# Two buffers by turns for the 16-bit tops of layer 1's weights

## The chip, the cores and the metric

The kernel runs on one core of a Trainium2 chip. Its time is the device time of one execution in microseconds (us); three runs of the kernel before gave 930.24, 930.90 and 930.96, median 930.9. Each engine of the core works through a queue of its own, in order: TensorE (PE in the rows; PEld is its weight loads), VectorE (DVE), ScalarE (ACT), GpSimd (POOL) and SyncE (SP), which only issues DMAs here. An instruction that waits holds up all that stands behind it on its engine.

## The reference

An attention block with exponential features, and behind it two feed-forward layers, each 512 to 2048 to 512 wide, over 2304 tokens:

```
q_p, k_p = phi(q_s), phi(k_s)          # phi(x) = exp(h - max(h)) / sqrt(m), h = x omega^T - |x|^2/2
num = q_p (k_p^T v);  den = q_p sum(k_p);  x = num / den       # 4 batches x 8 heads, 576 tokens
h = x @ w_in;  x = (h * clip(h + 3, 0, 6) / 6) @ w_out         # layer 1
h = x @ w_in;  out = (h / (1 + exp(-1.702 h))) @ w_out         # layer 2
```

## The kernel before

**Weights.** The weights reach the kernel as 64-bit floats, laid out in 16 chunks for each layer; a chunk holds 128 columns of w_in ("i") and 128 rows of w_out ("o"). For each chunk the kernel makes 32-bit floats, and splits these into a rounded part and a rest, since TensorE multiplies every product as three rounded ones. In the code l = 0 is layer 1 and l = 1 is layer 2. The conversion of a chunk is a chain over four engines:

- `convert_1`: ScalarE takes the top 16 bits of each word into `wtop` (L183) and the middle 32 bits into `w` (L185). VectorE works on `wtop` (L187 into `wmag`, L191 in place, L195 into `wpow`). GpSimd multiplies `w` by `wpow`, in two halves (L200).
- `convert_2`: VectorE adds `wtop` to `w` (L207), ScalarE rounds the half (L210), VectorE takes the rest (L211). The first half is the chunk's w_in, the second its w_out. L207 is the last reader of `wtop`.

`wtop` is a tile of 128x1024 16-bit values with a tag; tiles of one tag share its buffers. For l = 0 the tag is `wtop0` for every chunk, with one buffer, so L183 of a chunk can't start until both L207 of the chunk before are done. For l = 1 the tags `wtop0` and `wtop1` alternate. `wmag` and `wpow` have one buffer, `w`, the raw chunk `wraw` two, and the split weights go to a ring of six buffers (`wss`) or to eight that are kept (`wsh`).

**The work around it.** Layer 1 is done by 16 units for each batch: `emit_h` of a chunk is twelve products of 128x512 (L506), whose result ScalarE and VectorE gate and split into `gs` (L517, L518, L522, L523), and `emit_o` two units later adds the chunk's part of the output, twelve products (L556). Batch 0's units run while the weights are converted for the first time, two chunks ahead in the program's text; between them TensorE has the attention of batch 1 (projections L256, transposes L380, L432 and L439, L358 and L394 for the sums and quotients, with norms on VectorE, L416 to L421, and features, L267 and L269). The last quarter of a batch's attention reaches layer 1 through L432, L250 (ScalarE) and L251 (VectorE), which write the rows of `x` that every unit's last three products read.

**What sets the order.** The order on each engine is not the order of the text: when the program is built, a scheduler goes through a timeline of its own and lets each engine take what is ready there. So a change of buffers can move instructions on every engine, up to where the two timelines meet again.

Of the kernel before, what the change touches and what calls it, by code (L numbers as in the profile page):

```python
# [13 lines left out]
BF16 = mybir.dt.bfloat16  # L14
# [8 lines left out]
def performer_moe_kernel(  # L23
# [18 lines left out]
    B, NPAIR, P = qk.shape[:3]  # L42
# [25 lines left out]
    wp = wctx.enter_context(tc.tile_pool(name="wp", bufs=1))  # L68
# [23 lines left out]
    def behind(*ins):  # L92
        stack = ExitStack()
        for i in ins:
            if i is not None:
                stack.enter_context(tc.issue_after(i.ins))
        return stack
# [72 lines left out]
    def convert_1(l, c, act=None, dve=None):  # L170
        t = wraw.pop((l, c)).rearrange("p (w s) -> p w s", s=4)
        n = 2 * DM
        top = t[:, 1:n + 1, 0]
        mid = t.rearrange("p w s -> p (w s)").bitcast(U32).rearrange("p (w s) -> p w s", s=2)[:, 0:n, 1]
        a = wp.tile([P, n], BF16, tag=f"wtop{l and c % 2}", bufs=1, name="wtop")
        m = wp.tile([P, n], BF16, tag="wmag", bufs=1, name="wmag")
        q = wp.tile([P, n], BF16, tag="wpow", bufs=1, name="wpow")
        w = wp.tile([P, n], F32, tag="w", bufs=2, name="w")

        ab, mb, qb = a.bitcast(I32), m.bitcast(I32), q.bitcast(I32)  # L180
        act = act if isinstance(act, tuple) else (act, act)
        with behind(act[0]):
            nc.scalar.activation(out=a, in_=top.bitcast(BF16), func=AF.Copy, scale=2.0 ** -112)  # L183
        with behind(act[1]):
            nc.scalar.activation(out=w, in_=mid, func=AF.Copy, scale=2.0 ** -36)  # L185
        with behind(dve):
            nc.vector.tensor_scalar(  # L187
                out=mb, in0=ab, scalar1=3, scalar2=0x7FF87FF8,
                op0=ALU.logical_shift_left, op1=ALU.bitwise_and,
            )  # L190
            nc.vector.scalar_tensor_tensor(  # L191
                out=ab, in0=ab, scalar=-0x7FFF8000, in1=mb,
                op0=ALU.bitwise_and, op1=ALU.bitwise_or,
            )
            nc.vector.tensor_scalar(  # L195
                out=qb, in0=ab, scalar1=-0x7F0080, scalar2=None, op0=ALU.bitwise_and
            )
        for j in range(2):
            cols = slice(j * DM, (j + 1) * DM)
            nc.gpsimd.tensor_tensor(out=w[:, cols], in0=w[:, cols], in1=q[:, cols], op=ALU.mult)  # L200
        half[l, c] = a, w
# [512 lines left out]
    def convert_next(stage, upto, act=None, dve=None):  # L714

        while n_conv[stage - 1] < min(upto, len(conv)):
            if stage == 1:
                prefetch_w()
                convert_1(*conv[n_conv[0]], act, dve)
            else:  # L720
                convert_next(1, n_conv[1] + 1, act, dve)
                convert_2(*conv[n_conv[1]])
            n_conv[stage - 1] += 1
        prefetch_w()
# [96 lines left out]
    for u in range(len(units) + LAG):  # L821
        while fetches and fetches[0][0] <= u + AHEAD:
            fetch_w(0, *fetches.pop(0)[1:])
        if u < len(units):
            n, c = units[u]
# [373 lines left out]
```

## Time and profile before

| | us |
|---|---|
| median of the runs | 930.9 |
| the profiled execution | 930.89 |
| its span, first to last instruction | 929.1 |
| TensorE busy | 914.1 (98%) |
| VectorE, ScalarE, GpSimd busy | 585.9, 481.5, 334.4 |
| granted TensorE clock | 1.00, in every slice of the span |

Batch 0's units of layer 1 with the conversion of layer 1's weights take the stretch from about 36 to 176 us; before it stands the attention of batch 0, behind it the units of batches 1 to 3, then layer 2. An engine's busy time counts what its instructions hold, also where two matmuls overlap or an instruction is held up while it runs. A number in square brackets behind a row is idle time of the engine, with what ended it.

### The profile page before, as it was taken

Reading aid. Unit: us, or ns where it says so; the run is one execution under the profiler, and the core shown is the slowest. Engines: PE = TensorE matmul, PEld = TensorE weight load, DVE = VectorE, ACT = ScalarE, POOL = GpSimd, SP = SyncE. Lnnn points to the kernel's source line nnn. Section 1 sums busy time; section 2 is a strip of 40 time slices with the busy share of each in tenths; the row PEclk is TensorE's granted clock in tenths of the full one; section 3 lists DMA queues with packets and bytes.
Section 4 is the critical chain, followed back from the end, with each engine's and each line's share of the span. In section 5 each row is a group of like instructions: output and inputs, shape, how many; then the busy total and the mean of one; then the engine's idle time right before and its main releaser. Section 6 shows DMA issues by size and latency. Waiting matters only on the chain.

```text
span 929.1 us, 16457 instructions
## 1 busy us (share of the span) xinstructions
PE 914.1 (98%) x6274; PEld 782.1 (84%) x6274; DVE 585.9 (63%) x980; ACT 481.5 (52%) x977; POOL 334.4 (36%) x283
## 2 busy tenths in 40 slices
PE   8999999999999999999999999999999999999998
PEld 6877777778887888878888888878999888899997
DVE  5888889587585766727643433766875443377653
ACT  6977676476665665636533333444544223244443
POOL 0122222077573547544772112784000244420000
PEclk9999999999999999999999999999999999999999
DMA  6677777889878887766765426999889654566672
GB/s 210 241 250 250 238 248 268 293 297 339 307 271 277 287 319 288 261 238 234 265 239 191 137 93 224 369 405 316 275 285 333 199 175 159 176 187 183 169 261 92
DMA packets 75167, 228.77 MB, mean 246 GB/s; under 512 B 7504, under 2 KB 13264, under 8 KB 75088
## 3 DMA queue, kind: packets, MB, share of 16 engines
q1 hardware_dynamic: 74928, 227.45, 71.2%
q8 instruction: 50, 0.82, 0.3%
q10 hardware_dynamic: 160, 0.26, 0.1%
q14 instruction: 29, 0.24, 0.1%
HBM read 164.77 MB, written 62.91 MB: 245 GB/s over the span
## 4 chain that ended last, share of the span: by engine, by line
PE 84%; DVE 9%; ACT 3%; POOL 2%; issue 1%; DMA 1%; POOLq 0%; DVEq 0%; ACTq 0%
PE o L1003 19%; PE ps L506 18%; PE o L556 18%; PE h L872 16%; PE ps L261 3%; PE hl L889 2%; DVE w L207 2%; PE ps L394 1%; PE ps L256 1%; PE ps L358 1%; DVE gs L523 1%; PE ps L380 1%; POOL w L200 1%; DVE wtop L191 1%; ACT e L269 1%
## 5 line engine op out<-in xcount | busy, mean ns | idle before, releaser
L506 PE MATMUL ps<-x,wss 128*128 128x512 f32 x768 | 193.9, 397 | 3.3 <-ACT wss L210 1.8
L1003 PE MATMUL o<-wss,gs 128*128 128x256 f32 x1536 | 185.4, 283 | 0.3
L1003 PEld LDWEIGHTS o<-wss,gs 128*128 128x128 f32 x1536 | 184.6, 191 | 1.2 <-DVE gs L974 0.5
L506 PEld LDWEIGHTS ps<-x,wss 128*128 128x128 f32 x768 | 139.4, 188 | 35.4 <-ACT wss L210 3.7
L872 PE MATMUL h<-xo,wss 128*128 128x512 f32 x672 | 160.0, 394 | 0.4 <-DVE t L905 0.4
L200 POOL TENSOR_TENSOR w<-w,wpow 128x512 f32<-128x512 f32 x64 | 78.1, 1240 | 202.1 <-DVE wpow L195 123.6
L872 PEld LDWEIGHTS h<-xo,wss 128*128 128x128 f32 x672 | 124.1, 188 | 28.1 <-DVE t L905 0.8
L913 POOL TENSOR_TENSOR g<-g,c 128x512 f32<-128x512 f32 x48 | 64.5, 1346 | 170.3 <-ACT g L912 170.0
L973 ACT CAST gs<-g 128x512 fp32r<-128x512 f32 x112 | 69.4, 621 | 85.1 <-PE o L1003 79.3
L556 PE MATMUL o<-gs,wsh 128*128 128x512 f32 (+1 forms) x480 | 111.7, 377 | 0.3 <-ACT gs L522 0.3
L556 PE MATMUL o<-gs,wss 128*128 128x512 f32 (+1 forms) x480 | 109.4, 374 | 2.4 <-ACT gs L522 2.4
L974 DVE TENSOR_TENSOR gs<-g,gs 128x512 fp32r<-128x512 f32 x112 | 79.7, 716 | 47.8 <-ACT gs L973 45.0
L224 POOL TENSOR_TENSOR wsn<-w,wsn 128x512 fp32r<-128x512 f32 x64 | 90.5, 1429 | 48.8 <-ACT wsn L223 48.8
L518 DVE SCALAR_TENSOR_TENSOR ga<-ga,ps 128x512 f32<-128x512 f32 (+1 forms) x80 | 50.0, 629 | 91.3 <-ACT ga L517 91.1
L517 ACT ACTIVATE ga<-ps,three 128x512 f32<-128x512 f32 (+1 forms) x80 | 51.6, 650 | 94.1 <-PE ps L506 93.9
L556 PEld LDWEIGHTS o<-gs,wss 128*128 128x128 f32 x480 | 81.5, 188 | 17.3 <-ACT gs L522 3.3
L556 PEld LDWEIGHTS o<-gs,wsh 128*128 128x128 f32 x480 | 81.7, 188 | 16.2 <-ACT gs L522 1.0
L269 ACT ACTIVATE e<-ps,mx 128x128 f32<-128x128 f32 x220 | 62.2, 392 | 30.9 <-DVE mx L267 30.9
L523 DVE TENSOR_TENSOR gs<-ga,gs 128x512 fp32r<-128x512 f32 (+1 forms) x80 | 65.1, 824 | 19.4 <-ACT gs L522 18.1
L207 DVE TENSOR_TENSOR w<-w,wtop 128x512 f32<-128x512 f32 x64 | 65.5, 1033 | 10.6 <-POOL w L200 10.2
L912 ACT ACTIVATE g<-c 128x512 f32<-128x512 f32 x48 | 30.3, 632 | 60.3 <-DVE c L905 60.3
L223 ACT CAST wsn<-w 128x512 fp32r<-128x512 f32 x64 | 38.6, 626 | 27.3 <-issue 9.5
(146 smaller groups left out, 1184.1 us busy)
## 6 DMA issues: line engine op xcount, KB each, us to landing
wss<-left SPq DMA_DIRECT2D x64, 512.0 KB, 4.0
wss<-ws0i SPq DMA_DIRECT2D x48, 512.0 KB, 4.6
wraw<-in_w_in_dram SPq DMA_DIRECT2D x32, 512.0 KB, 4.8
wraw<-in_w_out_dram SPq DMA_DIRECT2D x32, 512.0 KB, 5.9
left<-wsn SPq DMA_DIRECT2D x32, 512.0 KB, 3.6
wss<-ws0o SPq DMA_DIRECT2D x24, 512.0 KB, 4.4
ws0i<-wss SPq DMA_DIRECT2D x16, 512.0 KB, 3.1
wss<-sumsa SPq DMA_DIRECT2D x16, 512.0 KB, 3.9
```

What stands on the lines that cost most here:

```text
L200: nc.gpsimd.tensor_tensor(out=w[:, cols], in0=w[:, cols], in1=q[:, cols], op=ALU.mult)
L207: nc.vector.tensor_tensor(out=wj, in0=wj, in1=a[:, j * DM:(j + 1) * DM], op=ALU.add)
L224: nc.gpsimd.tensor_tensor(out=s[:, :, 1], in0=t, in1=s[:, :, 0].bitcast(F32), op=ALU.subtract)
L269: act = nc.scalar.activation(out=e[:, r, :], in_=ps[:, r, :], func=AF.Exp, bias=mx[:, r:r + 1])
L506: nc.tensor.matmul(out=ps, lhsT=w[:, wi, kk, :], rhs=x[:, xi, kk, :], start=(m == 0), stop=(m == 3 * NK - 1),)
L523: gate[1] = nc.vector.tensor_tensor(out=s[:, 1, :], in0=g, in1=s[:, 0, :].bitcast(F32), op=ALU.subtract)
L556: nc.tensor.matmul(out=ps[:, e, :], lhsT=w[:, wi, cols], rhs=s[:, gi, :], start=(c == 0 and m == 0 and per == 1), stop=(c == NC - 1 and m ...
L872: nc.tensor.matmul(out=ps, lhsT=s[:, wi, q, :], rhs=xop[q, op][:, xi], start=(first and m == 0), stop=(m == 5), skip_group_check=not first,)
L913: mul = eng.tensor_tensor(out=g, in0=g, in1=src, op=ALU.mult)
L973: split_ins[0] = nc.scalar.copy(s[:, 0], g)
L974: split_ins[1] = nc.vector.tensor_tensor(out=s[:, 1], in0=g, in1=s[:, 0].bitcast(F32), op=ALU.subtract)
L1003: last_row[0] = nc.tensor.matmul(out=out, lhsT=s[:, gi, d * P:(d + 1) * P], rhs=w[:, wi, :], start=(start and m == 0), stop=(stop and m == 2),
```

## The change

The tag of `wtop` alternates for both layers, instead of for layer 2 alone. The second buffer exists already.

```
-        a = wp.tile([P, n], BF16, tag=f"wtop{l and c % 2}", bufs=1, name="wtop")
+        a = wp.tile([P, n], BF16, tag=f"wtop{c % 2}", bufs=1, name="wtop")
```

No instruction is added or removed; the scheduler's order changes on TensorE, VectorE, ScalarE and SyncE between about 37 and 178 us of the span before, and is the same from there to the end. GpSimd's is the same throughout.

The first place is TensorE's queue in the opening, where batch 0's attention ends. `ps_800`, `ps_889` and `ps_954` are the results of units 0, 1 and 2, `xt_726` the last quarter of batch 0's attention, `x0_196` layer 1's input. Before:

```order
L506 MATMUL ps_889<-x0_196,wss_880 128x512 x7
L256 MATMUL ps_908<-omt_166,qk_647 128x128 x4
L432 MATMUL acc_786<-ident_81,xt_726 128x128 x4
L439 MATMUL acc_793<-ident_81,xln_316 128x64 x3
L256 MATMUL ps_909<-omt_166,qk_647 128x128 x4
L439 MATMUL acc_793<-ident_81,xln_316 128x64
L506 MATMUL ps_800<-x0_196,wss_626 128x512
L506 MATMUL ps_889<-x0_196,wss_880 128x512
L506 MATMUL ps_800<-x0_196,wss_626 128x512 x2
L506 MATMUL ps_889<-x0_196,wss_880 128x512 x2
L506 MATMUL ps_954<-x0_196,wss_946 128x512 x12
```

After:

```order
L506 MATMUL ps_889<-x0_196,wss_880 128x512 x7
L256 MATMUL ps_909<-omt_166,qk_647 128x128 x4
L432 MATMUL acc_786<-ident_81,xt_726 128x128 x4
L439 MATMUL acc_793<-ident_81,xln_316 128x64 x3
L506 MATMUL ps_954<-x0_196,wss_946 128x512 x9
L506 MATMUL ps_800<-x0_196,wss_626 128x512
L506 MATMUL ps_889<-x0_196,wss_880 128x512
L506 MATMUL ps_954<-x0_196,wss_946 128x512
L439 MATMUL acc_793<-ident_81,xln_316 128x64
L380 MATMUL ps_973<-ident_81,e_829 128x128 x4
L506 MATMUL ps_800<-x0_196,wss_626 128x512 x2
L506 MATMUL ps_889<-x0_196,wss_880 128x512 x2
```

The four projections into `ps_908` stand ahead of the seven products now, those into `ps_909` ahead of the transposes; nine products of unit 2 come ahead of the ones that need the last rows of `x`. Behind this TensorE now has all of unit 3 and eight more projections before the first L556; before, the first L556 came ahead of unit 3.

The second place is VectorE's queue around the norm of that last quarter (`xt_726` from `den_776`), in the same opening. `wtop_931` and `w_934` belong to chunk 2, `wtop_980` to chunk 3. Before:

```order
L416 TENSOR_SCALAR den_776<-acc_765 128x4
L420 RECIPROCAL rden_778<-den_776 128x4
L187 TENSOR_SCALAR wmag_932<-wtop_931 128x512
L421 TENSOR_TENSOR xt_726<-acc_765,rden_778 128x4x64
L416 TENSOR_SCALAR den_781<-acc_765 64x2
L191 SCALAR_TENSOR_TENSOR wtop_931<-wtop_931,wmag_932 128x512
L420 RECIPROCAL rden_783<-den_781 64x2
L195 TENSOR_SCALAR wpow_933<-wtop_931 128x512
L421 TENSOR_TENSOR xln_316<-acc_765,rden_783 64x128
```

After:

```order
L416 TENSOR_SCALAR den_776<-acc_765 128x4
L211 TENSOR_TENSOR wss_885<-w_868,wss_885 128x512
L207 TENSOR_TENSOR w_934<-w_934,wtop_931 128x512
L420 RECIPROCAL rden_778<-den_776 128x4
L187 TENSOR_SCALAR wmag_981<-wtop_980 128x512
L267 TENSOR_REDUCE mx_919<-ps_908 128x4
L207 TENSOR_TENSOR w_934<-w_934,wtop_931 128x512
L421 TENSOR_TENSOR xt_726<-acc_765,rden_778 128x4x64
L416 TENSOR_SCALAR den_781<-acc_765 64x2
L191 SCALAR_TENSOR_TENSOR wtop_980<-wtop_980,wmag_981 128x512
L211 TENSOR_TENSOR wss_946<-w_934,wss_946 128x512
L267 TENSOR_REDUCE mx_925<-ps_909 128x4
```

The conversion stands a whole step further on at the same point: chunk 2 has its L207 here where it had its L187, and chunk 3 its L187. L191 and L195 of chunk 2 are further up now.

The third place is TensorE's queue in the middle of the stretch, at a unit in the second half of the 16. Before:

```order
L380 MATMUL ps<-ident,e 128x128 x4
L556 MATMUL o<-gs,wss 128x512 x12
L506 MATMUL ps<-x_196,wss 128x512 x2
L358 MATMUL ps<-v,e 64x65 x8
L366 MATMUL ps<-lv,el 64x65
L506 MATMUL ps<-x_196,wss 128x512 x10
```

After:

```order
L380 MATMUL ps<-ident,e 128x128 x4
L556 MATMUL o<-gs,wsh 128x512 x10
L506 MATMUL ps<-x_196,wss 128x512 x12
L358 MATMUL ps<-v,e 64x65 x8
L366 MATMUL ps<-lv,el 64x65 x2
```

Before, the first two products of a unit, which need only L210's rounded half of the weights, stand apart from the ten that need L211's rest too, with attention between them. After, the twelve of a unit follow each other.

## Rows read from the trace of the kernel before

**Rows 1.** The page: busy us of each engine, share of the span, instructions.
```profile
PE 914.1 (98%) x6274; PEld 782.1 (84%) x6274; DVE 585.9 (63%) x980; ACT 481.5 (52%) x977; POOL 334.4 (36%) x283
```

**Rows 2.** Windows: stretch and its length, each engine's busy us (instructions), clock, DMA share.
```profile
44.00:59.00 15.00, 14.58 (x111) 10.74 (x107) 13.23 (x29) 13.68 (x34) 2.33 (x3) 1.00 0.87 288
...
74.00:174.00 100.00, 95.90 (x680) 73.48 (x681) 84.82 (x157) 67.58 (x133) 25.12 (x22) 1.00 0.76 261
...
205.00:480.00 275.00, 274.85 (x1857) 225.69 (x1857) 176.60 (x293) 161.09 (x340) 168.60 (x151) 1.00 0.79 280
```

**Rows 3.** Waits of PE, 44 to 180 us: us in total, times, longest.
```profile
PE o L556 <- ACT gs L522: 2.7, 5, 1.2
PE ps L506 <- ACT wss L210: 1.8, 3, 1.2
PE ps L506 <- DVE wss L211: 0.4, 1, 0.4
```

**Rows 4.** Waits of PEld, 44 to 180 us.
```profile
PEld o L556 <- ACT gs L522: 4.3, 6, 1.4
PEld ps L506 <- ACT wss L210: 3.7, 5, 1.6
...
PEld ps L506 <- DVE wss L211: 0.9, 1, 0.9
```

**Rows 5.** Lines, PE, 44 to 180 us: busy, mean ns of one | idle before.
```profile
L506 PE MATMUL ps<-x,wss 128*128 128x512 f32 x195 | 52.4, 404 | 2.3 <-ACT wss L210 1.8 <-DVE wss L211 0.4
```

**Rows 6.** The chain of waits, 44 to 180 us: start, us, what.
```profile
76.30 2.74 PE ps L506 x12
```

**Rows 7.** Timeline of DVE, one chunk: start, us, instruction [idle before <-releaser].
```profile
143.89 0.43 DVE L187 TENSOR_SCALAR wmag<-wtop 128x512 int32<-128x512 int32 x1 [0.34 <-ACT wtop L183]
...
145.08 0.43 DVE L195 TENSOR_SCALAR wpow<-wtop 128x512 int32<-128x512 int32 x1
146.85 1.63 DVE L207 TENSOR_TENSOR w<-w,wtop 128x512 f32<-128x512 f32 x1 [1.34 <-POOL w L200]
...
149.00 0.68 DVE L207 TENSOR_TENSOR w<-w,wtop 128x512 f32<-128x512 f32 x1
149.60 0.68 DVE L211 TENSOR_TENSOR wss<-w,wss 128x512 fp32r<-128x512 f32 x1
```

**Rows 8.** Timeline of POOL, the same chunk.
```profile
145.65 2.28 POOL L200 TENSOR_TENSOR w<-w,wpow 128x512 f32<-128x512 f32 x2 [5.23 <-DVE wpow L195]
```

**Rows 9.** Timeline of ACT: L183 of this chunk and of the next.
```profile
142.73 1.13 ACT L183 ACTIVATE wtop<-wraw 128x1024 bf16<-128x1024 bf16 x1
...
150.24 1.11 ACT L183 ACTIVATE wtop<-wraw 128x1024 bf16<-128x1024 bf16 x1
```

**Rows 10.** Timeline of PE in the opening: last transposes of batch 0, first L556.
```profile
50.60 0.66 PE L432 MATMUL acc<-ident,xt 128*128 128x128 f32 x4
...
58.90 0.50 PE L556 MATMUL o<-gs,wsh 128*128 128x512 f32 x1
```

**Rows 11.** Timeline of DVE in the opening.
```profile
48.21 0.40 DVE L187 TENSOR_SCALAR wmag<-wtop 128x512 int32<-128x512 int32 x1
48.52 0.42 DVE L421 TENSOR_TENSOR xt<-acc,rden 128x256 f32<-128x256 f32 x1
...
51.91 0.69 DVE L251 TENSOR_TENSOR x<-acc,x 128x512 fp32r<-128x512 f32 x1 [0.51 <-ACT x L250]
```

**Rows 12.** Timeline of POOL where layer 2's weights are converted.
```profile
257.10 2.48 POOL L200 TENSOR_TENSOR w<-w,wpow 128x512 f32<-128x512 f32 x2 [5.70 <-DVE wpow L195]
```

**Rows 13.** Timeline of DVE, the same place.
```profile
257.41 1.14 DVE L187 TENSOR_SCALAR wmag<-wtop 128x512 int32<-128x512 int32 x1 [0.45 <-ACT wtop L183]
258.58 1.54 DVE L191 SCALAR_TENSOR_TENSOR wtop<-wtop,wmag 128x512 int32<-128x512 int32 x1
```

**Rows 14.** Timeline of PE, the projections of two heads of batch 1.
```profile
81.88 1.71 PE L256 MATMUL ps<-omt,qk 64*128 64x128 f32 x16
...
111.93 1.16 PE L256 MATMUL ps<-omt,qk 64*128 64x128 f32 x16
```

## The prediction

> **What bounds the kernel now.** I read the page first: TensorE is busy 98% of the span, so only its waits can be won [rows 1]. Next the windows: from 205 to 480 us it is busy 274.85 of 275, in the 100 us from 74 to 174 only 95.90, and there VectorE is at 84.82, in the opening (44 to 59) at 13.23 of 15 [rows 2]. The order is the same behind about 178 us, so whatever is gained or lost arises before that, and as TensorE is full afterwards it should reach the end unchanged.
>
> Then the waits of that stretch, twice. TensorE's matmuls sat idle 2.7 us for `gs` (five times) and 1.8 + 0.4 for the weights `wss` (four times), 4.9 in all [rows 3]. Its weight loads sat idle 4.3 + 3.7 + 0.9 = 8.9 for the same releasers [rows 4]. The truth lies between: a matmul counts as busy for 404 ns [rows 5], while in a full run of twelve one starts each 2.74 / 12 = 0.228 us [rows 6]; so each wait hides about 0.17 us in the busy time of the matmul before it. Nine waits give 4.9 + 9 x 0.17 = 6.4; I take 6.5. That is all there is to win here, 0.7% of the time.
>
> Last the timeline of one chunk. L183 starts at 142.73, L207's second half starts at 149.00, and the next chunk's L183 at 150.24, right behind it [rows 7, 9]. So a chunk is a chain of 7.5 us with no overlap with the next. On it VectorE idles 1.34 us for GpSimd and then its first L207 takes 1.63 instead of 0.68, because GpSimd's second product is still running (145.65 to 147.93) [rows 7, 8]. L211 is ready just when TensorE wants it: hence the unit split in two and ten products.
>
> **The change part by part.** *Removed.* L183 no longer waits for L207, so a chunk's L187 and L191 go under GpSimd's time of the chunk before. In the new order the twelve products of each unit stand together. In steady state L211 of a chunk stands on VectorE behind L518 of a unit two to four before it; it was one before. Between a unit's last L506 and its L556 the order now has 6 us or more of matmuls (counted at 0.228 each, attention added), where it had 2 to 4 in half of the units. Both kinds of wait lose their reason: -6.5, between -4.9 and -8.9.
>
> *TensorE's own work.* The count is unchanged. But a head's sixteen projections take 1.16 us where the two halves of the array alternate and 1.71 where each half has a block of eight [rows 14]. By the new order one more head has blocks, and part of a second: +0.6.
>
> *The opening.* Here the new order costs something. VectorE is nearly full, and the conversion has moved ahead of the end of batch 0's attention. Ahead of the norm `xt_726` (L421, at 48.52 before [rows 11]) it now also does L191 and L195 of chunk 2, both its L207, L187 of chunk 3 and one L267. Neighbours of 0.68 us start 0.60 apart (149.00, 149.60 [rows 7]), L187 and L421 0.31 (48.21, 48.52 [rows 11]); with 0.6 four times and 0.35 twice that is 3.1. Chunk 1 itself comes about 1.0 later, as ScalarE does chunk 2's L183 (1.13 [rows 9]) ahead of chunk 1's L185. And VectorE now meets GpSimd more often. Where layer 2's conversion already alternates, L187 and L191 took 1.14 and 1.54 us beside L200 [rows 12, 13], against 0.43 [rows 7]: each ends about half a microsecond after one of GpSimd's two products, and the second product gets longer, 2.48 against 2.28 for both [rows 8, 12]. So VectorE is let in between them and waits for the rest of one product, on average half of 1.16. Four such meetings before `xt_726` make 4 x 0.5 = 2.0, less the 0.95 that L207 pays now: +0.9 rounded down. L421 then starts near 53.5 and ends at 53.9. TensorE comes to the transposes (50.60 [rows 10]) about 1.4 later than now, with eight projections (0.9) moved ahead and 0.4 of waiting for unit 1's weights: 52.0. That is a new wait of 1.9. Behind it the nine products of unit 2 wait 0.4 for L211 of chunk 2, the last six products of units 0 to 2 about 0.3 for L251 (51.91 now, near 58 then), and unit 3 about 0.4: +3.0 in all. From below: without meetings and with chunk 1 on time, L421 starts at 48.52 + 3.1 = 51.6, ahead of TensorE, and 0.7 is left. From above: if VectorE had to sit out both products each time, four of those meetings lie on the path and cost 1.16 more each: 3.0 + 4.6 = 7.6. I take 3.0, as rows 13 show VectorE let in.
>
> The Trainium skill (SBUF — State Buffer, "Summary: rules for kernel authors") speaks against the change here: of a VectorE instruction with two SBUF inputs and a GpSimd one, the second to issue is blocked until the first has finished. The 1.54 us of L191 agree, and so does L207's 1.63; that the block ends with the one product and not with the pair is the row's, not the page's. By the rule alone, with GpSimd's second product queued first, the sum would be the upper one.
>
> *Behind the opening.* Unit 4 stands behind 31 L556 (7.1 us) and a quotient, so it is due near 75 us; its L211 stands nine VectorE instructions (5.4 us) behind that of chunk 3, which ends near 63, so it is ready near 69 with a meeting. From there VectorE's work is at most what it is now, 84.82 us in 100 [rows 2]. A full TensorE with its inputs ahead does not wait (0.15 in 275 us [rows 2]); for in-order accidents I put +0.5, between 0 and 1.5.
>
> *Sum.* 930.9 - 6.5 + 0.6 + 3.0 + 0.5 = 928.5. The profiled execution took 930.89, the median is 930.90, so nothing has to be shifted. The bounds together: 930.9 - 8.9 + 0.6 + 0.7 = 923.3 and 930.9 - 4.9 + 0.6 + 7.6 + 1.5 = 935.7; neither has all its ends at once.
>
> **The rivals.** *Slower: the opening takes it all.* One mechanism: VectorE sits out both of GpSimd's products, the last quarter of `x` and unit 3's weights come 4.6 us later, and TensorE, whose first L556 now stands behind unit 3, has nothing to go to. Time: 928.5 + 4.6 = 933.1. For it: VectorE at 13.23 of 15 in the opening [rows 2], and first L556 at 58.90 now [rows 10], near 67 by my sum. Against: rows 13. It decides from the point where the first L556 starts after 69.4 (my 67 plus the 2.4 to be won).
>
> *No change: `gs` stays late.* The five waits for `gs` come from L517 to L523, which share VectorE and ScalarE with the conversion; if those engines' queues hold them just as now, 2.7 + 5 x 0.17 = 3.6 is not won: 928.5 + 3.6 = 932.1, 0.13% above the present. For it: the same amount of VectorE work must fit into less time. Against: the 6 us or more that now stand between.
>
> *A larger gain.* The opening costs only its lower end: 928.5 - 2.3 = 926.2. For it: the scheduler placed the transposes where it thought their input ready.
>
> *It doesn't do what it says.* `wpow` still has one buffer, `w` and `wraw` two, and if one of them takes the place of `wtop` the chain keeps its 7.5 us: 930.9. Against: L195 of a chunk needs only L200 of the one before, and in the new order L187 stands ahead of the L207 of the chunk before.
>
> **How the numbers follow.** Forecast 0.43, larger gain 0.13, `gs` stays 0.21, slower 0.16, nothing 0.07. This kernel's runs tell a change from none at about 0.2%, 1.9 us. Faster than 929.0: the larger gain and most of the forecast (0.38 of it), 0.51. Slower than 932.8: the slower rival and a little of the `gs` one, 0.17. The rest, 0.32, is the same. The range 925.8 to 932.6 holds the forecast, the gain and the two flat cases, and leaves out the worse part of the slower one; the forecast alone has 927.2 to 929.5.
>
> **What would show it.** In the profile after: L183 of a chunk ahead of the L207 of the one before; the waits of L556 for `gs` and of L506 for `wss` between 74 and 174 us below 1 us together; a wait of 1 to 3 us before L432 near 52 us; the first L556 between 65 and 69; L251 near 58; L187 or L191 over 1 us beside L200; the stretch behind 205 us as before, only earlier. Wrong would be a gain that arises behind 205 us, a first L556 before 64, or waits of over 2 us for `gs` that remain.

## The result and the profile after

The changed kernel takes 937.1 us (median of 4 runs, 936.6 to 937.4) against 930.6 for the kernel before on the same chip: 1.0069 times as long, 95% interval 1.0057 to 1.0082. I had forecast 928.5 and a range up to 932.6, so it is slower, outside the range, and the sign is wrong too. The profiled execution took 936.6 us, its span is 934.7 (929.1 before).

First the windows, as in [rows 2]: stretch, length, busy us of PE, PEld, DVE, ACT, POOL, then the granted clock.

```profile
44.00:59.00 15.00, 14.28 (x106) 10.73 (x105) 15.00 (x30) 13.66 (x35) 7.21 (x5) 1.00 0.95 351
59.00:74.00 15.00, 13.84 (x84) 10.76 (x83) 15.00 (x24) 13.64 (x26) 5.38 (x5) 1.00 0.75 264
74.00:174.00 100.00, 94.16 (x668) 72.38 (x668) 82.92 (x144) 63.17 (x121) 30.57 (x21) 0.98 0.71 247
210.00:485.00 275.00, 274.85 (x1857) 225.64 (x1856) 176.13 (x293) 160.96 (x340) 168.60 (x151) 1.00 0.79 280
```

From 210 us on the order is the same and TensorE as full as before; its work comes 5.0 us later there. Another 1.2 us goes where layer 2 begins, near 600 us, and that is not the change's doing: p4 and p9_one below, both with one buffer, lose 0.5 and 1.2 us there too beside this trace of the kernel before. In the stretch that was to win, TensorE has lost 1.7 us more than before (94.16 for 95.90), and its clock is 0.98 for 1.00. VectorE has been full for the 30 us before it. Between 74 and 174 us it is busy for less time than before (82.92 for 84.82).

The waits of PE from 44 to 180 us, which answer to [rows 3] (us in total, times, longest):

```profile
PE ps L380 <- DVE wtop L191: 1.8, 1, 1.8
PE ps L380 <- DVE ga L518: 1.6, 2, 1.1
PE ps L506 <- DVE ga L518: 1.2, 1, 1.2
PE ps L432 <- DVE den L416: 1.0, 1, 1.0
PE acc L432 <- DVE den L416: 0.7, 1, 0.7
PE ps L506 <- DVE xln L421: 0.7, 1, 0.7
PE ps L506 <- DVE xt L421: 0.4, 1, 0.4
PE ps L506 <- ACT e L269: 0.3, 1, 0.3
```

All nine waits for `gs` and `wss` are gone, as forecast. In their place stand nine others, 7.7 us, none of them for weights. TensorE waits for what VectorE and ScalarE make of its earlier results: L518, L421, L416, L269. I call these the evictions: they empty PSUM banks or feed attention. The first row names a conversion instruction (L191) only because its semaphore came last; TensorE's weight load at that place waited 2.24 us for the exponentials L269:

```profile
125.80 0.42 PEld L380 LDWEIGHTS ps<-ident,e 128*128 128x128 f32 x4 [2.24 <-ACT e L269]
```

Why they are late shows in VectorE's timeline ahead of the longest wait (it answers to [rows 7], several chunks now mixed):

```profile
116.83 1.33 DVE L187 TENSOR_SCALAR wmag<-wtop 128x512 int32<-128x512 int32 x1
118.20 1.53 DVE L191 SCALAR_TENSOR_TENSOR wtop<-wtop,wmag 128x512 int32<-128x512 int32 x1
119.65 1.28 DVE L207 TENSOR_TENSOR w<-w,wtop 128x512 f32<-128x512 f32 x2
120.85 0.41 DVE L195 TENSOR_SCALAR wpow<-wtop 128x512 int32<-128x512 int32 x1
121.19 0.67 DVE L518 SCALAR_TENSOR_TENSOR ga<-ga,ps 128x512 f32<-128x512 f32 x1
...
122.99 1.27 DVE L267 TENSOR_REDUCE mx<-ps 128x4 f32<-128x512 f32 x2
```

and GpSimd's and ScalarE's beside it:

```profile
116.72 2.46 POOL L200 TENSOR_TENSOR w<-w,wpow 128x512 f32<-128x512 f32 x2 [5.11 <-DVE wpow L195]
```

```profile
116.72 0.69 ACT L517 ACTIVATE ga<-ps,three 128x512 f32<-128x512 f32 x1 [0.53 <-PE ps L506]
```

L517 ended at 117.40, so L518 could have run then. It ran at 121.19, 3.79 us later, behind five conversion instructions, of which L187 took 1.33 instead of 0.42 and L191 1.53 instead of 0.68, because GpSimd's two products ran from 116.72 to 119.18. I call that a meeting. The two meetings make 1.8 of the 3.79 us; the rest is the instructions' usual time. L267 behind it came 4.3 us after its input (the projections L256 ended at 118.65). ScalarE's queue has a part in this wait too: the first maximum was there at 123.7, but L269 started at 124.61, behind two conversion instructions (L185, L210).

VectorE's instructions by line, 38 to 181 us (busy, mean ns of one), show the meetings of the whole stretch. After:

```profile
L207 DVE TENSOR_TENSOR w<-w,wtop 128x512 f32<-128x512 f32 x30 | 26.2, 878 | 1.1 <-POOL w L200 1.1
L211 DVE TENSOR_TENSOR wss<-w,wss 128x512 fp32r<-128x512 f32 x23 | 21.1, 919 | 0.0
L191 DVE SCALAR_TENSOR_TENSOR wtop<-wtop,wmag 128x512 int32<-128x512 int32 x15 | 12.2, 811 | 0.1
L187 DVE TENSOR_SCALAR wmag<-wtop 128x512 int32<-128x512 int32 x15 | 10.3, 689 | 0.3 <-ACT wtop L183 0.3
```

Before:

```profile
L207 DVE TENSOR_TENSOR w<-w,wtop 128x512 f32<-128x512 f32 x30 | 32.7, 1102 | 10.0 <-POOL w L200 9.8
L211 DVE TENSOR_TENSOR wss<-w,wss 128x512 fp32r<-128x512 f32 x23 | 15.5, 679 | 0.2
L191 DVE SCALAR_TENSOR_TENSOR wtop<-wtop,wmag 128x512 int32<-128x512 int32 x15 | 10.3, 687 | 0.3
L187 DVE TENSOR_SCALAR wmag<-wtop 128x512 int32<-128x512 int32 x15 | 6.3, 419 | 2.8 <-ACT wtop L183 2.8
```

Before, only L207 met GpSimd, once a chunk, at a place where VectorE waited for GpSimd anyway (9.8 us). Now L187, L191 and L211 meet it too, and VectorE waits for L200 only once, 1.1 us. Adding up what each instruction took over its usual time gives 12.7 us before and 19.1 after.

### The profile page after: what moved, and what is told of

It is laid out like the page before. It is cut to its first block, busy times and chain, and to the rows that moved or that the text cites. A ratio compares the mean times of both kernels' runs of the same rounds, so it can differ in the third digit from the quotient of the medians.

```text
span 934.7 us, 16465 instructions
## 1 busy us (share of the span) xinstructions
PE 916.0 (98%) x6274; PEld 783.8 (84%) x6274; DVE 590.3 (63%) x980; ACT 481.6 (52%) x977; POOL 344.2 (37%) x283
## 4 chain that ended last, share of the span: by engine, by line
PE 82%; DVE 12%; ACT 2%; issue 1%; DMA 1%; POOL 1%; DVEq 0%; ACTq 0%
PE o L1003 19%; PE o L556 18%; PE ps L506 18%; PE h L872 15%; PE ps L261 3%; PE hl L889 2%; DVE w L207 2%; DVE wss L211 2%; PE ps L394 1%; DVE mx L267 1%; PE ps L358 1%; DVE wtop L191 1%; PE ps L380 1%; DVE wmag L187 1%; DVE gs L523 1%
## 5 line engine op out<-in xcount | busy, mean ns | idle before, releaser
L506 PE MATMUL ps<-x,wss 128*128 128x512 f32 x768 | 191.7, 396 | 3.5 <-DVE ga L518 1.4
L200 POOL TENSOR_TENSOR w<-w,wpow 128x512 f32<-128x512 f32 x64 | 88.4, 1401 | 197.1 <-DVE wpow L195 133.7
L556 PE MATMUL o<-gs,wsh 128*128 128x512 f32 (+1 forms) x480 | 114.1, 382 | 0.0
L973 ACT CAST gs<-g 128x512 fp32r<-128x512 f32 x112 | 69.4, 621 | 85.1 <-PE o L1003 79.3
L518 DVE SCALAR_TENSOR_TENSOR ga<-ga,ps 128x512 f32<-128x512 f32 (+1 forms) x80 | 50.0, 629 | 98.2 <-ACT ga L517 98.1
L556 PE MATMUL o<-gs,wss 128*128 128x512 f32 (+1 forms) x480 | 109.4, 373 | 0.0
L517 ACT ACTIVATE ga<-ps,three 128x512 f32<-128x512 f32 (+1 forms) x80 | 51.4, 647 | 92.2 <-PE ps L506 92.0
L556 PEld LDWEIGHTS o<-gs,wsh 128*128 128x128 f32 x480 | 82.8, 191 | 15.6
L556 PEld LDWEIGHTS o<-gs,wss 128*128 128x128 f32 x480 | 81.7, 188 | 14.4
L269 ACT ACTIVATE e<-ps,mx 128x128 f32<-128x128 f32 x220 | 62.5, 389 | 34.1 <-DVE mx L267 34.1
L207 DVE TENSOR_TENSOR w<-w,wtop 128x512 f32<-128x512 f32 x64 | 59.0, 928 | 1.7 <-POOL w L200 1.5
L522 ACT CAST gs<-ga 128x512 fp32r<-128x512 f32 (+1 forms) x80 | 45.9, 580 | 13.6 <-DVE ga L518 13.4
```

The costliest lines, as they stand in the source:

```text
L207: nc.vector.tensor_tensor(out=wj, in0=wj, in1=a[:, j * DM:(j + 1) * DM], op=ALU.add)
L269: act = nc.scalar.activation(out=e[:, r, :], in_=ps[:, r, :], func=AF.Exp, bias=mx[:, r:r + 1])
L506: nc.tensor.matmul(out=ps, lhsT=w[:, wi, kk, :], rhs=x[:, xi, kk, :], start=(m == 0), stop=(m == 3 * NK - 1),)
L556: nc.tensor.matmul(out=ps[:, e, :], lhsT=w[:, wi, cols], rhs=s[:, gi, :], start=(c == 0 and m == 0 and per == 1), stop=(c == NC - 1 and m ...
L973: split_ins[0] = nc.scalar.copy(s[:, 0], g)
```

## The experiments

Two theories stood at the start. *Order*: with the second buffer the scheduler puts conversions ahead of evictions, and the evictions are late whatever GpSimd does. *Port*: the conversions are in the way because their meetings with GpSimd take time that the order did not reckon with (I did not look into the scheduler's own timeline, so that it leaves them out is inferred). A third, the rival of the prediction, puts the loss into the opening.

To change one thing at a time I fixed the order. At the end of the program each engine's instructions get edges of issue order (no waits) from a table:

```
+def pin(tc, table):
+    for engine, places in table.items():
...
+        tc.add_manual_dep(own[k], prev.name, <order only>, reason="pin")
```

Every ratio is to the kernel before, run beside it (its medians were 930.5 to 930.9), and can differ from the quotient of the medians by 0.1%. The changed kernel with its own order fixed and nothing else edited was not run; p1 shows for the other order that fixing costs nothing that can be seen. Where an edit adds a line, lines behind 200 read one higher than above.

**The second buffer in the old order** (p1).

```
-        a = wp.tile([P, n], BF16, tag=f"wtop{l and c % 2}", bufs=1, name="wtop")
+        a = wp.tile([P, n], BF16, tag=f"wtop{c % 2}", bufs=1, name="wtop")
+        pin(tc, ORDER)   # the order of the kernel before
```

> Two buffers for wtop, but every engine issues its instructions in exactly the order of the kernel before (edges of issue order, no waits). Order theory (the loss comes from where the scheduler put the conversion once it had two buffers): 930.6 like the kernel before, within 0.1%. Port theory (the loss comes from VectorE and GpSimd meeting more often): 930.6 too, since the meetings come with the order. If the second buffer itself costs something (its place in SBUF, its waits): 932 to 937.

931.2 us, ratio 1.0002 (0.9993 to 1.0011). The buffer itself, and the fixing, cost at most 1.0 us, the upper end of the interval; the loss comes with the new order. Both theories stand.

**Evictions first** (p2): the changed kernel with VectorE's and ScalarE's tables rewritten between 62 and 176 us.

> The changed kernel with its orders of TensorE, GpSimd and the DMA queue, but between 62 and 176 us VectorE and ScalarE take what empties PSUM (L267, L416 to L421, L518, L523, L269, L517, L382, L374, L250 and L251) ahead of conversion instructions that started after its input was there; the conversion keeps its own order and is at most about 1.2 us later. Order theory: the new waits of L380, L432 and L506 for these lines (6.6 us between 74 and 174) and the slow clock behind the longest (1.6) go: 929 to 931.5. Port theory: VectorE still meets GpSimd as often and is as late: 934 to 937.

942.2 us, ratio 1.0117 (1.0102 to 1.0133): worse still, and outside both ranges. The new waits of PE from 74 to 174 us:

```profile
PE o L556 <- ACT gs L522: 4.4, 1, 4.4
PE ps L358 <- ACT qpt L382: 1.9, 1, 1.9
PE ps L506 <- ACT kv L374: 1.5, 1, 1.5
PE ps L256 <- ACT kv L374: 1.3, 1, 1.3
```

Putting evictions ahead by this table did not make them early. My table took each input's time from a trace in which VectorE was late; with other times the two in-order engines stood waiting for each other and for transfers (ScalarE 2.7 us for the words of one chunk, with evictions queued behind). The run decides for neither theory, since it changed more than I meant.

**Short products in the new and in the old order** (p3, p4).

```
+            cols = slice(j * DM, j * DM + DM // 4) if l == 0 else cols
             nc.gpsimd.tensor_tensor(out=w[:, cols], in0=w[:, cols], in1=q[:, cols], op=ALU.mult)
```

> The changed kernel with all its orders fixed, but GpSimd's products L200 of layer 1 work on 128 of their 512 columns each (the other three quarters of the product are left out), so that VectorE hardly meets GpSimd. Port theory: the 6.4 us that VectorE lost more than before come back and the time falls to 931 or below. Order theory: the evictions stand behind the same conversion instructions, of which some are shorter: the stalls at 110 and 126 us with the slow clock (1.2 + 2.0 + 1.6) remain and only those behind a stretched instruction (81, 91, 101, 136 us: 0.5 + 0.7 + 0.9 + 1.2 = 3.2) go: about 934.

924.5 us, ratio 0.9922 (0.9910 to 0.9935).

> The kernel before, its orders fixed, with the same shortened L200 (three quarters of the product of layer 1 left out), as the price of the same edit in the old order. Its chain of 7.5 us per chunk gets some 2 us shorter (1.34 of idle and 0.95 of stretched L207), so both theories expect most of its waits for wss and gs to go: 924 to 928. Were the waits not from this chain: 930.6.

927.6 us, ratio 0.9961 (0.9948 to 0.9975). In the changed kernel's own order, p3 is 12.6 us faster than it. Its shorter products also reach VectorE earlier, but VectorE's only wait for L200 was the 1.1 us above, so nearly all of this is the meetings. From 74 to 174 us (columns as above):

```profile
74.00:174.00 100.00, 100.00 (x715) 78.73 (x714) 71.15 (x146) 61.31 (x122) 10.79 (x18) 1.00 0.75 261
```

TensorE has no wait left. So even the stalls at 110 and 126 us, which had no meeting right ahead of them and which I had given to the order, were the meetings' work, carried along VectorE's queue. The same instructions as in the timeline above, in p3:

```profile
107.27 0.63 DVE L187 TENSOR_SCALAR wmag<-wtop 128x512 int32<-128x512 int32 x1
107.93 0.80 DVE L191 SCALAR_TENSOR_TENSOR wtop<-wtop,wmag 128x512 int32<-128x512 int32 x1
108.66 1.28 DVE L208 TENSOR_TENSOR w<-w,wtop 128x512 f32<-128x512 f32 x2
109.86 0.41 DVE L195 TENSOR_SCALAR wpow<-wtop 128x512 int32<-128x512 int32 x1
110.87 0.69 DVE L519 SCALAR_TENSOR_TENSOR ga<-ga,ps 128x512 f32<-128x512 f32 x1 [0.59 <-ACT ga L518]
```

Here VectorE waits for L518's input instead of coming 3.79 us late. From 74 to 174 us, the start of L267 lies behind the last semaphore update that it waits for by 1.71 us on average before, 3.46 in the changed kernel, 0.57 in p3; that of L518 by 0.75, 1.61 and 0.59. And p3 is 3.2 us under p4: where GpSimd is out of the way, the change gains, and about half of the 6.5 us that I had put on the waits.

**Where the meetings hurt** (p5 and p6): the same edit with `l == 0 and c < 4`, and with `l == 0 and c >= 4`.

> The changed kernel with all its orders fixed, and L200 shortened to 128 of 512 columns in chunks 0 to 3 of layer 1 alone (there three quarters of the product are left out): VectorE meets GpSimd no more in the opening, but as before behind it. If the meetings in the opening are the loss (my rival of the prediction): 931 or below. If those behind it are: only the stalls at 43, 54 and 62 us get smaller (3.0 us in the changed kernel, 0.6 where every product is short), so about 934.5.

933.5 us, ratio 1.0032 (1.0020 to 1.0043).

> The same with the short products in chunks 4 to 15 alone (three quarters of their products left out). If the meetings behind the opening are the loss: the seven stalls between 74 and 178 us (6.8) and the slow clock behind one of them (1.6) go, 937.1 - 8.4 = 928.7, and 927 to 930 with what the opening's end gains. If those in the opening are: 935 or more.

927.1 us, ratio 0.9966 (0.9953 to 0.9979). The meetings behind the opening are worth 937.1 - 927.1 = 10.0 us, those in it 3.6. The opening is the place of the smaller part of the loss.

**Half products** (p10): `DM // 2` in place of `DM // 4`.

> The changed kernel with all its orders fixed, and all 32 products of layer 1 on 256 of their 512 columns (half of each product left out). If the loss goes with the time that VectorE stands beside GpSimd: near the middle of 924.5 (128 columns) and 937.1 (512), by columns 937.1 - 12.6 x 2/3 = 928.7. If there is slack that takes up small delays: 925 to 926.

924.5 us, ratio 0.9931 (0.9918 to 0.9943), just below the range for slack and the same as with quarters, though the meetings still lengthen VectorE's instructions by 6.2 us (1.3 in p3). The loss does not go by columns: this order takes up 6 us of it, and somewhere between that and 19.1 it reaches TensorE.

**The product on VectorE** (p7), **fused with the scaling** (p8), **from chunk 2** (p9c) and **from chunk 4** (p9), complete kernels:

```
+            eng = nc.vector if l == 0 else nc.gpsimd        # p9: l == 0 and c >= 4
-            nc.gpsimd.tensor_tensor(out=w[:, cols], ...
+            eng.tensor_tensor(out=w[:, cols], ...
```

> Two buffers, and layer 1's product L200 on VectorE instead of GpSimd, nothing left out, order by the scheduler. VectorE gets 32 products of about 0.60 us (19.2), as much as its meetings with GpSimd cost it in the changed kernel (19.1), but spread as the scheduler knows it, and a product is 0.6 long where GpSimd took 1.16 or more. If VectorE's sum of work is what counts: 934 to 938, like the changed kernel. If it is that the meetings fall where the scheduler did not expect them: 927 to 931. If the length of GpSimd's part of a chunk's chain counts beside that: 925 or below.

930.5 us, ratio 1.0009 (0.9992 to 1.0026). From 74 to 174 us:

```profile
74.00:174.00 100.00, 100.00 (x705) 79.27 (x703) 82.07 (x170) 63.49 (x123) 0.00 (x0) 1.00 0.72 252
```

VectorE is as busy as in the changed kernel (82.07 for 82.92) and TensorE never waits. So VectorE's sum of work alone is not what costs. What p7 loses in this execution, it loses in the opening (one wait of 2.3 us for ScalarE's L374). The execution took 929.0 us; p7's twelve lie between 928.2 and 936.7, and what the longer ones lose was not traced.

> As p7_product_dve, and the scaling of the middle words (L185 on ScalarE, 1.12 us a chunk) goes into the same VectorE instruction, so ScalarE has 16 x 1.12 = 18 us less in the stretch; nothing left out. If ScalarE's queue takes part in the lateness of the evictions (L517 and L382 stand behind conversion there): 1 to 2 us below p7_product_dve. If VectorE alone sets it: the same as p7_product_dve. If a scalar_tensor_tensor with strided words takes longer than 0.60 us: above it.

931.1 us, ratio 1.0005 (0.9997 to 1.0014): not below p7. It does not settle ScalarE's part, though. From 74 to 174 us p7 had no wait left to win (p8: 99.88), and from 44 to 59 p8, in an order made anew, has TensorE busy for only 12.64 us at a clock of 0.89, where p7 has 13.78 at 1.00.

> Two buffers, the product on VectorE from chunk 2 on. Between p7_product_dve (930.5) and p9_dve_from_4: if VectorE's load in the opening (nearly full there) is what makes p7's opening stall 4.9 us, about 930; if the meetings of chunks 2 and 3 with GpSimd cost more than that load, below p9_dve_from_4.

928.1 us, ratio 0.9971 (0.9960 to 0.9981), below both p7 and p9; but the scheduler made each of these orders anew, so it does not tell which of the two reasons holds.

> Two buffers; the product L200 of layer 1 stays on GpSimd for chunks 0 to 3 and is on VectorE for chunks 4 to 15, nothing left out, order by the scheduler. If only the meetings behind the opening cost: the opening as in the changed kernel (stalls of 3.0 us), nothing behind it: 937.1 - 6.8 - 1.6 = 928.7, some 2 us under p7_product_dve, whose opening stalls 4.9. If the sum of VectorE's work decides: 933 or more.

931.0 us, ratio 0.9993 (0.9983 to 1.0002), 2 us above what I expected: the scheduler's new order stalls in the opening, where the clock also falls (0.50 from 66 to 68 us), and has three short waits from 130 to 134 us (1.2 us).

**The same with one buffer** (p9_one): the edit of p9 in the kernel before.

> The same with the one buffer of the kernel before for layer 1. If the second buffer is worth something where GpSimd is out of the way: 1 to 4 us above p9_dve_from_4 (the two kernels with short products differ by 3.2). If a chain with the product on VectorE (L183, L187, L191, L195, two L200, two L207: about 1.1 + 0.3 + 0.3 + 0.6 + 0.3 + 1.2 + 1.2 = 5 us instead of 7.5) is short enough for TensorE's 6.9 us a unit: the same as p9_dve_from_4.

925.95 us, ratio 0.9946 (0.9933 to 0.9958): not above p9 but 5 us below it, and the fastest complete kernel here. From 74 to 174 us:

```profile
74.00:174.00 100.00, 100.00 (x709) 78.34 (x706) 87.44 (x178) 67.08 (x132) 0.00 (x0) 0.99 0.78 272
```

TensorE is full with VectorE at 87.44, more than in any other kernel here. The first L556 comes at 57.97, as early as before. Here the chain of a chunk is short enough without a second buffer.

**Two last questions** (p11, p12): the meetings themselves, or any work that the order does not know of? And the buffer, or the order, between p9 and p9_one?

```
+            eng = nc.vector if l == 0 else nc.gpsimd
+        pin(tc, ORDER)   # p11: the changed kernel's, L200 put into VectorE's queue where GpSimd began it
```

> The changed kernel with its orders of TensorE, ScalarE and the DMA queue fixed, and with the 32 products of layer 1 on VectorE, each put into VectorE's fixed order at the place where GpSimd began it in the changed kernel; nothing left out. VectorE has 32 x 0.60 = 19.2 us more of its own work in place of the 19.1 us that it lost to meetings, again in an order made without it. If any unplanned 19 us on VectorE do it: 934 to 938, with stalls of TensorE for the same evictions. If it needs the meetings (which fall on an eviction's predecessors and hold VectorE up to 1 us at once): 931 or below.

933.7 us, ratio 1.0034 (1.0024 to 1.0045). VectorE meets GpSimd nowhere in this stretch, and yet PE waits from 40 to 174 us, in four of these five rows for what it waits for in the changed kernel too (lines one higher):

```profile
PE ps L381 <- ACT e L270: 1.7, 1, 1.7
PE o L557 <- ACT gs L523: 1.6, 1, 1.6
PE acc L395 <- ACT kv L375: 1.1, 1, 1.1
PE ps L381 <- DVE ga L519: 0.9, 1, 0.9
PE ps L507 <- DVE xln L422: 0.4, 1, 0.4
```

Three lie where the changed kernel stalls, near 101, 110 and 126 us; the 1.6 for `gs`, near 134, is new. From 74 to 174 us:

```profile
74.00:174.00 100.00, 95.45 (x676) 74.23 (x676) 83.35 (x169) 64.94 (x123) 0.00 (x0) 0.98 0.71 249
```

So behind the opening TensorE loses nearly as much without a meeting as in the changed kernel (94.16 at 0.98). This execution took 937.3 us, 3.6 more than the median; its clock was 0.50 from 44 to 52 us. The time falls between my two ranges, so neither theory has it alone: 19 us of VectorE work in an order made without them cost 9.2 us against p3's 924.5, and the meetings, whose 19.1 us come in pieces of up to 1 us, 12.6.

> Two buffers, product on VectorE from chunk 4, as p9_dve_from_4 (931.0), but every engine in the order of p9_one (925.95). If the second buffer itself costs nothing and the order decides: 926, within 0.1%. If the second buffer costs by itself: up to 931.

927.2 us, ratio 0.9953 (0.9940 to 0.9966), with an interval that overlaps p9_one's. Most of the 5 us between p9 and p9_one is the order's; the medians differ by 1.2 us, and whether the buffer has a part in that is not resolved.

## Why the prediction was wrong, step by step

**What bounds the kernel, and what is removed: the mechanism right, the size open.** The nine waits are gone. p3, with 924.5 us, is 6.4 below the kernel before, but 3.2 of that come from the shorter products even with one buffer (p4), so it is no clean measure of the 6.5.

**TensorE's own work: too small.** From 36 to 182 us the projections L256 take 14.0 us on TensorE after 12.8 before: +1.2 for +0.6.

**The opening: right in place; that its size came near is partly luck.** L421 was to start at 53.5 and the transposes to wait 1.9. After ([rows 10, 11] before), on VectorE and on PE:

```profile
53.13 0.41 DVE L421 TENSOR_TENSOR xt<-acc,rden 128x256 f32<-128x256 f32 x1
...
56.87 0.68 DVE L251 TENSOR_TENSOR x<-acc,x 128x512 fp32r<-128x512 f32 x1
```

```profile
53.60 0.66 PE L432 MATMUL acc<-ident,xt 128*128 128x128 f32 x4 [0.72 <-DVE den L416]
...
61.79 0.70 PE L506 MATMUL ps<-x,wss 128*128 128x512 f32 x2 [1.16 <-DVE ga L518]
...
67.50 0.71 PE L556 MATMUL o<-gs,wsh 128*128 128x512 f32 x2
```

L421 and L251 came within half a microsecond and 1.1 us of the forecast, the first L556 at 67.5 for 67. The wait at L432 was 0.7 and not 1.9; instead unit 3 waited 1.16 for L518's bank where I had 0.4. The opening's meetings are worth 3.6 us (p5). That is near my 3.0 for the whole opening, but only 0.9 of the 3.0 stood for meetings; the rest was work moved ahead, and with every product short the opening's one stall is 0.6. Two slips are small: 2.0 less 0.95 is 1.05, and the two meetings of rows 13 end 0.28 and 0.55 us behind a product, not half a microsecond each. The slower rival, decided by a first L556 after 69.4, did not happen: the kernel is slower for another reason.

**Behind the opening: the step that failed.** I gave it +0.5, at most 1.5, with the words "A full TensorE with its inputs ahead does not wait". p6 prices the meetings there at 10.0 us, and p11 shows that as much other work on VectorE, unknown to the order, does most of the damage too (9.2 of 12.6 us over the whole kernel). In the changed kernel's trace it is seven stalls, 6.8 us from one matmul's start to the next beyond the usual, and 1.7 of slow clock (below). Three things were wrong in it. I counted only weights as inputs: TensorE also needs its four `ps` banks emptied, by instructions that stand in the same queues as the conversion. I compared VectorE's sum of work (at most 84.82 us in 100) with the stretch; the sum was right, 82.92, and says nothing, as p7 and p9_one show. And I priced the meetings in the opening alone, where I had found four, though rows 13 said that each L187 or L191 beside L200 takes 0.7 to 0.85 us more, all along the stretch. Putting 10.0 for 0.5 into my sum gives 928.5 - 0.5 + 10.0 = 938.0, against 937.1 measured. That is closer than the terms deserve: with 1.2 for TensorE's own work and 3.6 for the opening it is 939.2, and the two prices of meetings, 10.0 and 3.6, make 13.6 where removing all of them gave 12.6.

**The rule of the skill that I weighed** (the Trainium skill, SBUF — State Buffer, "Summary: rules for kernel authors") was the right warning at the wrong place: it bore on every chunk, not on four instructions of the opening. L191 above (1.53 us beside L200) agrees with it. L187 was held up as well (1.33), though it has one SBUF input and not the two of the rule as I quoted it.

**The other rivals.** `gs` stays late: no, that wait is gone. "It doesn't do what it says": no, the waits for the weights are gone as well. The larger gain did not come either. The changed kernel is slower, as the slower rival said, but not by its mechanism.

## What to carry to other kernels

A buffer that lets a scheduler overlap more also puts the overlapped work into other engines' in-order queues: check who stands behind it, evictions as much as weights, and whether the order knows what that work takes when engines get in each other's way. Here 6 us of unplanned time on VectorE cost nothing and 19 cost 9 to 13, so a price per meeting multiplied by their number is no estimate. Here, shortening the chain (product from chunk 4 on VectorE, one buffer) gave 0.54% where the second buffer cost 0.69%.

## What the runs showed of the hardware

TensorE's clock fell behind a short wait. Windows of the changed kernel around the 1.80 us wait at 124 to 125.8 (PE busy is the first number behind the length; the clock stands behind POOL):

```profile
124.00:126.00 2.00, 0.20 (x3) 0.20 (x3) 2.00 (x5) 2.00 (x8) 1.72 (x1) 1.00 1.04 299
126.00:128.00 2.00, 2.00 (x9) 1.61 (x9) 0.94 (x2) 2.00 (x6) 2.00 (x2) 0.60 1.01 297
128.00:130.00 2.00, 2.00 (x7) 1.57 (x6) 2.00 (x4) 1.27 (x3) 0.56 (x1) 0.55 0.97 346
130.00:132.00 2.00, 2.00 (x10) 1.64 (x9) 2.00 (x6) 1.28 (x2) 1.14 (x1) 1.00 1.02 418
```

For most of the 4 us from 126 on the engine ran at the lower of its two levels, 1.2 GHz, which costs 2 x (1 - 0.60) + 2 x (1 - 0.55) = 1.7 us, nearly as much as the wait itself. Before, a wait of 1.19 us near 122 left the clock at 1.00. In p11 a wait of 1.12 us near 42 did not: behind it the clock was 0.50 from 44 to 52 us. So the length of one wait alone does not tell whether the clock falls.

GpSimd pays for the meetings too: its 30 products between 38 and 181 us took 1,162 ns on average before, 1,503 in the changed kernel.

```profile
L200 POOL TENSOR_TENSOR w<-w,wpow 128x512 f32<-128x512 f32 x30 | 44.5, 1503 | 65.5 <-DVE wpow L195 51.8 <-ACT w L185 11.3 <-DVE den L416 2.3
```
